# A shorter head, new layout limits and a clock term in the layout model, in a 32-head attention kernel on Trainium2

## The chip, the cores and the metric

The kernel runs on one core of one Trainium2 chip. The metric is the device time of one execution in microseconds (us). The span that a profile covers is about 1.8 us shorter than the time of the same execution (744.4 against 746.23 us for the kernel before). Profiles are therefore compared with profiles, and times with times.

Engines are called as the profile calls them: PE is the TensorE matmul array, PEld its weight loads, DVE is VectorE, ACT is ScalarE, POOL is GpSimd, SP is SyncE, which issues most of the DMA here. L1821 is a line of the kernel's file; the line numbers shift by 11 between the kernel before and the changed one.

## The reference, cut to what matters

```python
x = A_x                                   # 1 x 2048 x 512, bf16
g = sigmoid((x * gate_w).sum(-1, keepdims=True))
# branch A: full attention, 32 heads of 16, 2048 queries x 2048 keys
q, k, v = split_heads(x @ A_wqkv)
a = softmax(q @ k.T * 0.25) @ v           # per head
a = merge_heads(a) @ A_wo
# branch B: the same shapes, but each query sees 8 keys, 2 apart (a sliding window)
b = ...
return g * a + (1 - g) * b
```

Branch A has 32 x 2048 x 2048 exponentials, and these are what costs time. Branch B is spread among them.

## The kernel before

A *tile* is the scores of 128 keys against 512 queries of one head: one matmul that writes 128x512 fp32 of PSUM, a *bank* in the kernel's words. There are 32 x 16 x 4 = 2048 tiles. Each has to be exponentiated, in one of two ways:

```python
# on ScalarE: 2 or 3 tiles in one instruction (1024 or 1536 wide); one value matmul per tile later
nc.scalar.activation(out=self.pt[a][i][:, 0:n * 512], in_=<score bank(s)>, func=ACT.Exp, scale=SCALE)

# on VectorE: one eviction per tile to int16 (an exponential by bit pattern), then three passes per
# batch of four tiles, each shifted by a constant; FOUR value matmuls per tile later
nc.vector.tensor_scalar(out=self.yb[buf][:, 0, i*512:(i+1)*512], in0=bank[:], scalar1=A, scalar2=B, ...)
nc.vector.tensor_scalar(out=y[:, k, 0:n], in0=y[:, 0, 0:n], scalar1=<constant k>, op0=ALU.add)   # k = 1, 2, 3
```

Nothing waits at run time for a decision: the *layout*, that is, which tile goes to which engine and in what order every engine does its work, is chosen when the kernel is built. `run()` plays the five engines forward in a model of time and always lets the engine that is behind do its best next step. Its rules have 11 limits (how much VectorE backlog is allowed before another tile is given to it, how long a group of value matmuls may be put off, and so on). Each limit has a value for each of the 64 stretches of 32 tiles:

```python
STRETCH = dict(
    backlog="2222233122222220322224220212223212210222223222422222222222223122",
    grab="2222232222222221442241322222132342122242322222222122222222222222",
    # [cut: nine more]
)
PE_0, DVE_0, ACT_0, SLOT_0, K_0 = 1.25, 2.7, 1.3, 1.45, 2.1   # when the model thinks each engine is free
WARM_WIN, WARM_BAR, WARM_LOW = 3.42, 3500, 2900

def slow(now):       # the model's view of TensorE's clock: slower only while it is starved
    return 1.9 if now > 15 and sum(n for a, n in work if a > now - WARM_WIN) < WARM_LOW else 1.0
```

When TensorE has had little work, `run()` inserts *fillers*, matmuls by a zero weight that add nothing to the bank they go to.

The head prepares the first tile: transposes of the first 512 rows of x, projection of q, and projection of the first 512 keys in two parts, because the first scores need only 128 of them. Both parts go to the same PSUM bank, `flex[0]`:

```python
def head(self):
    # [cut: warm-up matmuls, 16 transposes of x, 4 copies to xT, 16 q matmuls]
    for a, b in ((0, 128), (128, 512)):
        for kc in range(4):
            self.mm4(self.flex[0][:, a:b], lambda c: wk[:, kc, 32*c:32*c+32], self.xT[:, kc, a:b], ...)
        if a == 0:
            nc.scalar.activation(out=self.qm[0][0][:], in_=self.flex[1][:], func=ACT.Copy, ...)
        nc.vector.tensor_copy(out=self.kT[0][:, a:b], in_=self.flex[0][:, a:b])
    # [cut]

# setup, on VectorE, before the head: masks that are needed only much later
nc.vector.tensor_scalar(out=pidx[:], in0=pidx[:], scalar1=4, ..., op0=ALU.arith_shift_right)
nc.vector.tensor_copy(out=pf[:], in_=pidx[:])
nc.vector.tensor_copy(out=ef, in_=ei)                          # 128x128 int32 to f32
nc.vector.tensor_scalar(out=self.Eh[:], in0=ef, ..., op0=ALU.is_equal)
nc.vector.tensor_reduce(out=self.fold[:], in_=<ident>, ..., op=ALU.max)

# jobs: the v projection of chunk st may start at tile 4*st; for st = 0 that is ahead of the first scores
ch = self.chain([("PE", ..., v_mm), ("DVE", ..., v_evac)], due=..., rel=4 * st, deps=xs[st // 4])
```

## Time and profile before

Six runs took 744.41 to 745.88 us, median 745.22. The table is worked out from the trace of the profiled run.

| what | before |
|---|---|
| busy: ACT / PE / DVE, us | 725.9 / 703.1 / 692.2 |
| first exponential starts | 9.34 us |
| last exponential starts | 733.60 us |
| exponentials: 1024-wide / 1536-wide | 474 / 209 (1575 tiles) |
| tiles on VectorE | 473 |
| filler matmuls | 96 |

From start to start, when nothing is in its way, ACT takes 0.905 us for a 1024-wide exponential, 1.332 us for a 1536-wide one and 0.477 us for the few 512-wide copies that it also does. I add these up from the first to the start of the last exponential and call the sum the *base* (710.7 us). What the real distances have above it is the *excess* (13.5 us). Base, excess, the start of the first exponential, and the *tail* (from the start of the last exponential to ACT's last output issue, 5.6 us) account for the span but for about 5 us behind that issue (its transfer lands after 3.1 us; then the program ends).

The first lines are from the page of the kernel before: the span, the busy time of each engine with its share, and the granted clock of TensorE in tenths over 40 slices of the span.

```profile
span 744.4 us, 21345 instructions
...
PE 703.1 (94%) x8673; PEld 232.3 (31%) x8673; DVE 692.2 (93%) x1176; ACT 725.9 (98%) x697; POOL 204.4 (27%) x212
...
PEclk9999999999999999999989999999998999999999
```

ACT is the bound, with 98%. PE and DVE are at 94% and 93%. The two 8s in the last row are the slices in which TensorE's clock was halved for a while (granted clock 0.50 for 10.24 us from 384.2 and for 6.83 us from 565.1).

The timeline of the kernel before, cut to the head. Columns: start, duration, engine, line, operation, out<-in, shapes, count, and in brackets the idle time before it and what ended that.

```profile
2.13 2.80 DVE L845 CAST t_96<-t_96 128x128 f32<-128x128 int32 x1
...
5.45 1.08 DVE L937 COPY xT<-fps 128x512 bf16<-128x512 bf16 x3
...
7.35 0.29 DVE L948 CAST kT_72<-fps 128x128 bf16<-128x128 f32 x1 [0.82 <-PE fps L865]
7.70 0.83 PE L865 MATMUL fps<-xT,ww 128*32 128x384 bf16 x16 [0.39 <-DVE kT_72 L948]
...
8.34 0.63 PE L865 MATMUL fps<-wAv,xT 128*32 128x128 bf16 x32
8.58 0.56 DVE L948 CAST kT_72<-fps 128x384 bf16<-128x384 f32 x1 [0.93 <-PE fps L865]
...
8.91 0.40 PE L1767 MATMUL fps<-qm_0_74,kT_72 32*128 32x512 bf16 x4
...
9.34 1.02 ACT L1821 ACTIVATE pt_0_83<-fps 128x1024 bf16<-128x1024 f32 x1 [1.52 <-PE fps L1767]
```

The 128 keys are evicted at 7.35. PE waits 0.39 us for that eviction, though its next matmuls need nothing from it: they write the same bank. Then come 16 matmuls for the other keys, 32 for v, and only then the first scores (8.91), although what these need was there at about 7.65. ACT waits until 9.34.

The table by stretches of the kernel before, around the first halved clock. Columns: stretch, its length, busy time and count on PE, PEld, DVE, ACT and POOL, granted clock, DMA share, GB/s.

```profile
380.00:382.00 2.00, 1.07 (x15) 0.33 (x13) 2.00 (x5) 2.00 (x3) 0.00 (x0) 1.00 0.03 8
...
384.00:386.00 2.00, 1.77 (x11) 0.44 (x11) 1.93 (x5) 2.00 (x3) 0.00 (x0) 0.54 0.57 225
...
388.00:390.00 2.00, 2.00 (x14) 0.24 (x9) 2.00 (x5) 2.00 (x2) 0.00 (x0) 0.50 0.09 30
...
392.00:394.00 2.00, 2.00 (x23) 0.35 (x20) 1.10 (x2) 1.69 (x3) 0.00 (x0) 0.50 0.42 136
394.00:396.00 2.00, 2.00 (x35) 0.57 (x27) 1.97 (x4) 2.00 (x2) 0.00 (x0) 0.90 0.44 140
```

PE is busy only 1.07 of 2 us at 380 to 382; from about 384 its clock is 0.50. At first ACT does not notice (2.00 of 2.00 busy). At 392 it does: 1.69, while PE, with its clock at 0.50, starts 23 matmuls in 2 us, where 394 to 396 has 35 at 0.90.

### The profile page before, as it was taken

How to read it: one execution, taken by the hardware profiler on the slowest of the kernel's cores; microseconds unless marked ns; L12 is line 12 of the kernel's file. 1: busy time of each engine (PE TensorE's matmuls, PEld its weight loads, DVE VectorE, ACT ScalarE, POOL GpSimd, SP SyncE). 2: the span in 40 equal slices, each digit the busy share in tenths (PEclk: the TensorE clock that was granted, in tenths of full speed). 3: DMA queues.
4: the chain of work that ended last, by engine and by line, in shares of the span. 5: the costliest groups of instructions: out<-in, count | busy, mean ns of one | idle time of the engine just before them, and what ended most of it. 6: DMA issues, size and time to landing. Idle time of an engine off the chain costs nothing.

```text
span 744.4 us, 21345 instructions
## 1 busy us (share of the span) xinstructions
PE 703.1 (94%) x8673; PEld 232.3 (31%) x8673; DVE 692.2 (93%) x1176; ACT 725.9 (98%) x697; POOL 204.4 (27%) x212
## 2 busy tenths in 40 slices
PE   9999999999999999999989999999999999999996
PEld 5422332333322333232222233223322223233443
DVE  6999999997999999999998999999999998989995
ACT  6999999999999999999999999999999999999995
POOL 2053000000002232231003446556543555553000
PEclk9999999999999999999989999999998999999999
DMA  5012001001000100001042655465534556531001
GB/s 164 3 22 60 9 3 29 2 2 38 2 6 11 23 1 9 2 1 37 9 131 83 155 135 146 116 155 146 139 96 119 139 138 147 141 85 31 17 23 34
DMA packets 63722, 48.58 MB, mean 65 GB/s; under 512 B 21760, under 2 KB 63232, under 8 KB 63488
## 3 DMA queue, kind: packets, MB, share of 16 engines
q1 hardware_dynamic: 62912, 45.70, 23.7%
q8 instruction: 70, 1.15, 0.7%
q0 software_dynamic: 288, 1.05, 0.4%
q10 hardware_dynamic: 416, 0.39, 0.2%
q14 instruction: 36, 0.29, 0.2%
HBM read 39.85 MB, written 5.26 MB: 61 GB/s over the span
## 4 chain that ended last, share of the span: by engine, by line
ACT 47%; PE 32%; issue 14%; DVE 4%; SPq 2%; DMA 1%; ACTq 0%; DVEq 0%
PE fps L1767 11%; PE fps L1573 10%; PE fps L865 9%; ACT pt_2_85 L1821 6%; ACT pt_0_87 L1821 6%; ACT pt_0_83 L1821 6%; ACT pt_1_84 L1821 6%; ACT pt_2_89 L1821 6%; ACT pt_1_88 L1821 6%; ACT pt_3_86 L1821 6%; ACT pt_3_90 L1821 5%; DVE yb_91 L1502 1%; SPq L922 1%; DVE yb_93 L1508 1%; SPq L1269 1%
## 5 line engine op out<-in xcount | busy, mean ns | idle before, releaser
L1573 PEld LDWEIGHTS <-vaug 128*32 128x32 bf16 x3685 | 85.8, 95 | 134.0 <-issue 110.9
L1821 ACT ACTIVATE pt_0_83<-fps 128x1536 bf16<-128x1536 f32 (+1 forms) x86 | 117.9, 1371 | 1.9 <-PE fps L1767 1.8
L1821 ACT ACTIVATE pt_1_84<-fps 128x1536 bf16<-128x1536 f32 (+1 forms) x86 | 117.9, 1371 | 0.8 <-PE fps L1767 0.6
L1821 ACT ACTIVATE pt_2_85<-fps 128x1536 bf16<-128x1536 f32 (+1 forms) x85 | 118.1, 1389 | 0.5 <-PE fps L1767 0.3
L1821 ACT ACTIVATE pt_3_86<-fps 128x1536 bf16<-128x1536 f32 (+1 forms) x85 | 116.4, 1370 | 0.5 <-PE fps L1767 0.5
L1502 DVE TENSOR_SCALAR yb_91<-fps 128x512 int16<-128x512 f32 x163 | 107.4, 680 | 8.2 <-PE fps L1767 7.8
L1502 DVE TENSOR_SCALAR yb_92<-fps 128x512 int16<-128x512 f32 x154 | 102.1, 682 | 6.6 <-PE fps L1767 6.2
L1502 DVE TENSOR_SCALAR yb_93<-fps 128x512 int16<-128x512 f32 x156 | 102.6, 681 | 4.6 <-PE fps L1767 4.3
L1573 PE MATMUL fps<-yb_91,vaug 128*32 128x512 f16 (+1 forms) x700 | 104.1, 372 | 0.3
L1573 PE MATMUL fps<-yb_92,vaug 128*32 128x512 f16 (+1 forms) x656 | 101.4, 370 | 0.0
L1573 PE MATMUL fps<-yb_93,vaug 128*32 128x512 f16 (+1 forms) x656 | 100.5, 381 | 0.0
L865 PE MATMUL fps<-xT,ww 128*32 128x512 bf16 (+2 forms) x1296 | 99.3, 381 | 0.6 <-DVE kT_72 L948 0.4
L1821 ACT ACTIVATE pt_1_88<-fps 128x1024 bf16<-128x1024 f32 x86 | 96.0, 1117 | 0.3 <-PE fps L1767 0.2
L1821 ACT ACTIVATE pt_0_87<-fps 128x1024 bf16<-128x1024 f32 x86 | 96.2, 1118 | 0.0
L1821 ACT ACTIVATE pt_2_89<-fps 128x1024 bf16<-128x1024 f32 x85 | 95.2, 1120 | 0.1
L1821 ACT ACTIVATE pt_3_90<-fps 128x1024 bf16<-128x1024 f32 x84 | 93.7, 1116 | 0.3 <-PE fps L1767 0.2
L1767 PEld LDWEIGHTS <-kT_73 32*128 32x128 bf16 x1024 | 45.9, 91 | 149.5 <-issue 147.3
L1767 PEld LDWEIGHTS <-kT_72 32*128 32x128 bf16 x1024 | 45.4, 91 | 148.1 <-issue 144.6
L1508 DVE TENSOR_SCALAR yb_91<-yb_91 128x2048 int16<-128x2048 int16 (+3 forms) x129 | 81.4, 658 | 0.2
L1508 DVE TENSOR_SCALAR yb_92<-yb_92 128x2048 int16<-128x2048 int16 (+3 forms) x129 | 78.9, 641 | 0.2
L1508 DVE TENSOR_SCALAR yb_93<-yb_93 128x2048 int16<-128x2048 int16 (+3 forms) x126 | 77.8, 651 | 0.3
L1170 POOL TENSOR_TENSOR prod_879<-bq_867,bk_868 128x512 bf16<-128x512 bf16 x32 | 34.2, 1074 | 105.7 <-DVE yb_92 L1508 47.8
(189 smaller groups left out, 1282.7 us busy)
## 6 DMA issues: line engine op xcount, KB each, us to landing
vw_5712<-v_dram SPq DMA_DIRECT2D x64, 128.0 KB, 3.1
vw_5713<-v_dram SPq DMA_DIRECT2D x64, 128.0 KB, 3.1
er<-er_dram SPq DMA_DIRECT2D x128, 64.0 KB, 2.9
erb_5708<-er_dram SPq DMA_DIRECT2D x64, 64.0 KB, 3.0
erb_5709<-er_dram SPq DMA_DIRECT2D x64, 64.0 KB, 2.9
out_dram<-ob SPq DMA_DIRECT2D x15, 128.0 KB, 2.5
ww<-in_B_wqkv_dram SPq DMA_DIRECT2D x12, 128.0 KB, 2.9
ww<-in_A_wqkv_dram SPq DMA_DIRECT2D x8, 128.0 KB, 3.0
```

Source lines behind the costliest of these rows:

```text
L865: self.nc.tensor.matmul(out=out_ps[32 * c:32 * c + 32, 0:n], lhsT=lhsT_of(c), rhs=rhs, start=start, stop=stop, tile_position=(0, 32 * c))
L922: self.nc.sync.dma_start(out=self.qm[i % NQM][r][k:k + 16, :], in_=self.qs[i % 2][k:k + 16, :])
L1170: return e.tensor_tensor(out=pr[m % 2][:, a:b], in0=bq[ct][:, a:b], in1=bk[ct][:, o + a:o + b], op=ALU.mult)
L1269: nc.sync.dma_start(out=st_["erb"][m % 4][32 * k + 16 * r:32 * k + 16 * r + 16], in_=_ap(src, src.offset, [[0, 16], [2 * WIN * 512, 4], [1 ...
L1502: return nc.vector.tensor_scalar(out=self.yb[bt["buf"]][:, 0, i * 512:(i + 1) * 512], in0=bank[:], scalar1=A, scalar2=1024.0 * (15.0 + PW_ ...
L1508: return nc.vector.tensor_scalar(out=y[:, k, 0:n], in0=y[:, 0, 0:n], scalar1=float(round(1024.0 * (PW_S[k] - PW_S[0]))), scalar2=None, op0 ...
L1573: nc.tensor.matmul(out=out, lhsT=v, rhs=r, start=start, stop=stop, tile_position=(0, 32 * j))
L1767: nc.tensor.matmul(out=dst, lhsT=self.kT[ct % 2][32 * j:32 * j + 32, kt * 128:(kt + 1) * 128], rhs=self.qm[(4 * ct + qc) % NQM][par][32 * ...
L1821: nc.scalar.activation(out=self.pt[pi[0]][pi[1]][:, 0:n * 512], in_=self.aslot[si][:, 0:n, :].rearrange("p a b -> p (a b)"), func=ACT.Exp, ...
```

## The change

The intent: start the first exponential earlier; make the layout model count TensorE as slow for a whole `WARM_WIN` after it was starved (this constant, `WARM_LOW` and the 1.9 are the file's own); and search the limits anew. Of that search only the result is in the file.

```diff
 STRETCH = dict(
-    backlog="2222233122222220322224220212223212210222223222422222222222223122",
+    backlog="2123241201224222222420224223121223222212044232222222222222223223",
     # [cut: all 11 rows are new]
-PE_0, DVE_0, ACT_0, SLOT_0, K_0 = 1.25, 2.7, 1.3, 1.45, 2.1
+PE_0, DVE_0, ACT_0, SLOT_0, K_0 = 1.6, 3.0, 1.75, 1.8, 2.35
-WARM_LOW = 2900
+WARM_LOW = 2750
@@ setup
-        nc.vector.tensor_scalar(out=pidx[:], ...)      # the five mask instructions
-        # [cut]
+    def heads(self):                                   # ... are now a method
+        # [cut: the same five instructions]
@@ head
-        for a, b in ((0, 128), (128, 512)):
+        for a, b, bank in ((0, 128, self.flex[3]), (128, 512, self.flex[0])):
             for kc in range(4):
-                self.mm4(self.flex[0][:, a:b], ...
+                self.mm4(bank[:, a:b], ...
@@ jobs
+        self.steps.append(Step("DVE", 0.9, self.heads, rel=24, due=30, cls=2))
-                            due=4 * st - 4 if st else -20, rel=4 * st, deps=xs[st // 4])
+                            due=4 * st - 4 if st else -20, rel=max(1, 4 * st), deps=xs[st // 4])
@@ run
-        fx_free = [K_0, DVE_0, INF, 0.0]
+        fx_free = [K_0, DVE_0, INF, 1.5]
         def slow(now):
-            return 1.9 if now > 15 and sum(n for a, n in work if a > now - WARM_WIN) < WARM_LOW else 1.0
+            nonlocal cold_until
+            if now > 15 and sum(n for a, n in work if a > now - WARM_WIN) < WARM_LOW:
+                cold_until = now + WARM_WIN
+            return 1.9 if now < cold_until else 1.0
```

So there are two parts: a *head* part (own bank, masks later, v behind the first scores) and a *layout* part (everything that follows from the new limits and the new model). The layout of the changed kernel has 1570 tiles on ACT instead of 1575, and 478 on VectorE instead of 473.

## The prediction

> **What bounds the kernel.** ScalarE. The page's busy table gives ACT 725.9 of 744.4 us (98%), PE 703.1 (94%), DVE 692.2 (93%). ACT runs its 683 exponentials almost without a gap from 9.34 us (first exponential in the timeline) to 734.7 us. From start to start a 1024-wide one takes 0.905 us and a 1536-wide one 1.332 us. Against these, the start-to-start distances lose about 12 us inside that stretch, in some 60 places, mostly 0.05 to 0.3 us. The rest is head (9.3 us) and tail (9.7 us).

> Two places stand out. In the table by stretches TensorE's granted clock is 0.50 at 384 to 394 us and at 565 to 572 us. [...] PE was busy only 1.07 of 2 us at 380 to 382. Around these ACT loses about 2.9 us together.

> **What the change does.**
> 1. Head. The 384 other keys get their own bank, so their matmuls no longer wait for the 128-key eviction (PE waits 0.39 us, from 7.31 to 7.70). The first v projection (32 matmuls, 0.63 us) moves behind the first scores. The head-mask setup (a 2.80 us cast beside GpSimd's memsets, then 0.29 and 0.36) moves later, so the first xT copy need not wait until 5.45; I think this gains little, as PE finishes its transposes only at 5.88. First scores near 8.0 instead of 8.91, first exponential near 8.4 to 8.5 instead of 9.34: 0.9 us, all on the critical path.
> 2. Mix. The built order has 1570 tiles exponentiated on ACT instead of 1575, and 478 instead of 473 on VectorE; ACT still has 683 exponentials, 204 wide instead of 209. That is 5 x 0.427 = 2.1 us less ACT. VectorE gets 5 more evictions and 3 more passes of about 0.65, 5 us in all, and had 52 us free.
> 3. Clock. Placing each kernel's PE order on the exponentials' measured spacing and counting matmul work per 3.4 us, I find a deep, long dip in the old order where the first slow stretch lies and another where the second lies. In the new order I find only brief shallow ones. So I expect no half-clock stretch, or a short one: 2.5 us (estimate).
> 4. Against it: about 19 more value-matmul slots, 10 more filler groups and 22 more single-tile score groups on PE, some 10 us of PE work by the old durations; vanished half-clock periods give most of that back. Some small ACT stalls may grow: 0.5 us.

> **Sum.** 745.2 - 0.9 - 2.1 - 2.5 + 0.5 = 740.2; I say 740.0 us, 8 in 10 between 737.0 and 743.0. Faster by over 2%: 0.02. Within 2%: 0.97. Slower by over 2%: 0.01.

> **What would show each step.** Timeline: first exponential at 8.3 to 8.6 us, no PE wait on the first kT copy, no early 2.8 us cast. ACT groups: 204 wide and 479 narrow. Stretches: clock 1.00 from 20 to 720 us. ACT's excess near 9 to 10 us rather than 12.

> **What would make it wrong.** The layout was searched with a model; the new order may starve TensorE where I see none, or make ACT wait for scores behind the added PE work, which would give the 5 us back. A brief dip may be enough to halve the clock. The gain could be larger if the new limits also remove many small stalls.

The 2.5 us for the clock was the author's estimate, from the 2.9 us that ACT loses around the two stretches at 0.50. The 3.4 us over which step 3 counts is the step in which the clock changes in the profile before: its halved stretches of 10.24 and 6.83 us are three and two times 3.41.

## The result, and the profile after

| | before | after |
|---|---|---|
| median of all runs, us | 745.50 (40 runs, 744.41 to 746.86) | 745.92 (20 runs, 744.59 to 747.47) |
| ratio, 95% interval | | 1.0009 (1.0003 to 1.0015) |
| busy: ACT / PE / DVE, us | 725.9 / 703.1 / 692.2 | 724.0 / 707.8 / 693.5 |
| first exponential starts | 9.34 | 8.58 |
| base (ACT's minimum) | 710.7 | 708.2 |
| excess | 13.5 | 16.3 |
| tail | 5.58 | 6.67 |
| exponentials 1024 / 1536 wide | 474 / 209 | 479 / 204 |
| filler matmuls | 96 | 133 |

Ratios here and below are the mean time of one kernel's fast runs over the mean of the other's in the same rounds, so they are not quite the ratio of the medians. The predicted 740.0 us (737 to 743) was wrong. The kernel is not faster; within a tenth of a per cent it is even slower.

The same three lines from the page of the changed kernel:

```profile
span 745.1 us, 21464 instructions
...
PE 707.8 (95%) x8728; PEld 235.6 (32%) x8728; DVE 693.5 (93%) x1184; ACT 724.0 (97%) x697; POOL 204.7 (27%) x212
...
PEclk9999999999999999999999999999999999999999
```

ACT has 1.9 us less to do, as was intended, and the span is not shorter. Both old dips of the clock are gone from the last row (a slice is 18.6 us, and 3.4 us at half clock still leave 0.91 of it, which is a 9).

The timeline of the changed kernel: first the head, then 12 to 16 us.

```profile
5.06 0.85 DVE L943 COPY xT<-fps 128x512 bf16<-128x512 bf16 x2 [3.09 <-PE fps L940]
...
7.59 0.29 DVE L954 CAST kT_72<-fps 128x128 bf16<-128x128 f32 x1 [0.83 <-PE fps L871]
...
8.11 0.40 PE L1778 MATMUL fps<-qm_0_74,kT_72 32*128 32x512 bf16 x4
8.24 0.56 DVE L954 CAST kT_72<-fps 128x384 bf16<-128x384 f32 x1 [0.36 <-PE fps L871]
8.58 1.02 ACT L1832 ACTIVATE pt_0_83<-fps 128x1024 bf16<-128x1024 f32 x1 [0.52 <-PE fps L1778]
...
9.17 0.63 PE L871 MATMUL fps<-wAv,xT 128*32 128x128 bf16 x32
...
12.57 1.03 ACT L1832 ACTIVATE pt_2_85<-fps 128x1024 bf16<-128x1024 f32 x1
...
12.70 1.05 PE L871 MATMUL fps<-xT,ww 128*32 128x512 bf16 x16
...
13.68 0.62 PE L963 MATMUL fps<-ident,x_in_119 128*128 128x128 bf16 x8
...
14.23 0.63 PE L871 MATMUL fps<-wAv,xT 128*32 128x128 bf16 x32
...
14.79 0.60 PE L1778 MATMUL fps<-qm_0_74,kT_72 32*128 32x512 bf16 x5
...
15.25 1.02 ACT L1832 ACTIVATE pt_2_89<-fps 128x1024 bf16<-128x1024 f32 x1 [1.65 <-PE fps L1778]
```

The head works as intended. The transposes of x begin at 4.39 us in both runs, but here they start about 0.107 us apart up to the last (5.99), where before they start 0.056 us apart from 5.32 on; the first change of the clock in the trace falls at 6.34 here and at 5.28 before. So the 128 keys are evicted 0.24 us *later* than before (7.59 against 7.35), and yet the scores start at 8.11 instead of 8.91 and the first exponential at 8.58 instead of 9.34. Directly behind it, however, there is a wait that the kernel before does not have: from 12.7 to 14.8 PE does a projection, eight transposes and v before the next scores, and ACT stands for 1.65 us. So 0.76 us are won at 8.6 us, and at first sight more than that is gone at 15.3 us.

The table by stretches of the changed kernel at 476 to 480 us, and from its timeline the exponential that paid for it.

```profile
476.00:478.00 2.00, 0.98 (x10) 0.25 (x13) 1.93 (x10) 2.00 (x3) 2.00 (x2) 0.84 0.20 42
478.00:480.00 2.00, 2.00 (x17) 0.56 (x16) 0.63 (x2) 1.62 (x2) 0.03 (x1) 0.50 0.13 33
```

```profile
480.95 1.45 ACT L1832 ACTIVATE pt_3_86<-fps 128x1536 bf16<-128x1536 f32 x1 [1.33 <-PE fps L1778]
```

There is a new short stretch of halved clock, 3.41 us from 477.4, and ACT then waits 1.33 us for scores.

The end, from the timeline of the kernel before and then of the changed one: the last exponential, VectorE's transpose of the last block of values, and the last output issue.

```profile
733.60 1.08 ACT L1821 ACTIVATE pt_3_86<-fps 128x1024 bf16<-128x1024 f32 x1
...
735.16 0.72 DVE L1596 STREAM_TRANSPOSE t_96<-fps 128x512 f32<-128x512 f32 x1 [2.61 <-PE fps L1573]
...
738.80 0.37 ACTq L1419 DMA_DIRECT2D out_dram<-eg  x1
```

```profile
733.07 1.46 ACT L1832 ACTIVATE pt_3_86<-fps 128x1536 bf16<-128x1536 f32 x1
...
735.30 0.72 DVE L1607 STREAM_TRANSPOSE t_96<-fps 128x512 f32<-128x512 f32 x1 [0.17 <-PE fps L1584]
...
739.37 0.37 ACTq L1426 DMA_DIRECT2D out_dram<-eg  x1
```

The changed kernel starts its last exponential 0.53 us earlier and ends 0.57 us later. Its last exponential is a wide one (1.46 instead of 1.08), and what follows it takes longer too.

Here is the ledger of the two profiles by place. "Excess" is split by where in the span it lies.

| | before | after | difference |
|---|---|---|---|
| first exponential | 9.34 | 8.58 | -0.76 |
| base | 710.7 | 708.2 | -2.5 |
| excess, 9 to 50 us | 1.28 | 3.17 | +1.9 |
| excess, 375 to 400 and 550 to 575 us (the old halved clock) | 3.38 | 1.66 | -1.7 |
| excess, 470 to 490 us (the new one) | 0.31 | 1.60 | +1.3 |
| excess, everywhere else | 8.5 | 9.9 | +1.3 |
| tail | 5.58 | 6.67 | +1.1 |
| rest | | | +0.1 |
| span | 744.4 | 745.1 | +0.7 |

The base falls by six times 0.427 us and not five, because the wide last exponential lies in the tail; 0.4 of the tail's 1.1 us is that same exponential. The table tells where the time is. It does not yet tell what causes what: that took experiments.

### The profile page after: what moved, and what is told of

The parts are those of the page before. It is cut to its first block, busy times and chain, and to the rows that moved or that the text cites. A ratio compares the mean times of both kernels' runs of the same rounds, so it can differ in the third digit from the quotient of the medians.

```text
span 745.1 us, 21464 instructions
## 1 busy us (share of the span) xinstructions
PE 707.8 (95%) x8728; PEld 235.6 (32%) x8728; DVE 693.5 (93%) x1184; ACT 724.0 (97%) x697; POOL 204.7 (27%) x212
## 4 chain that ended last, share of the span: by engine, by line
ACT 42%; PE 22%; DVE 14%; issue 13%; DMA 3%; SPq 3%; POOL 1%; ACTq 0%; DVEq 0%; POOLq 0%
PE fps L1778 8%; PE fps L1584 7%; ACT pt_3_86 L1832 6%; ACT pt_2_85 L1832 6%; ACT pt_0_83 L1832 6%; ACT pt_2_89 L1832 5%; PE fps L871 5%; ACT pt_0_87 L1832 5%; ACT pt_3_90 L1832 5%; ACT pt_1_88 L1832 5%; ACT pt_1_84 L1832 5%; DVE yb_92 L1513 2%; DVE yb_91 L1513 2%; DVE prod_822 L1177 2%; DMA vw_5740<-v_dram 1%
## 5 line engine op out<-in xcount | busy, mean ns | idle before, releaser
L1832 ACT ACTIVATE pt_0_83<-fps 128x1536 bf16<-128x1536 f32 (+1 forms) x87 | 119.4, 1372 | 1.4 <-PE fps L1778 1.0
L1832 ACT ACTIVATE pt_3_86<-fps 128x1536 bf16<-128x1536 f32 (+1 forms) x85 | 114.9, 1352 | 1.4 <-PE fps L1778 1.3
L1832 ACT ACTIVATE pt_2_85<-fps 128x1536 bf16<-128x1536 f32 (+1 forms) x85 | 116.0, 1364 | 0.1
L1832 ACT ACTIVATE pt_1_84<-fps 128x1024 bf16<-128x1024 f32 (+1 forms) x85 | 114.7, 1350 | 0.4 <-PE fps L1778 0.4
L1584 PE MATMUL fps<-yb_93,vaug 128*32 128x512 f16 (+1 forms) x672 | 101.5, 373 | 0.5 <-DVE vaug L899 0.5
L1584 PE MATMUL fps<-yb_91,vaug 128*32 128x512 f16 (+1 forms) x672 | 100.7, 370 | 0.8 <-DVE yb_91 L1519 0.7
L871 PE MATMUL fps<-xT,ww 128*32 128x512 bf16 (+2 forms) x1296 | 97.7, 380 | 0.0
L1584 PE MATMUL fps<-yb_92,vaug 128*32 128x512 f16 (+1 forms) x692 | 95.7, 368 | 0.2
L1519 DVE TENSOR_SCALAR yb_93<-yb_93 128x2048 int16<-128x2048 int16 (+2 forms) x126 | 81.0, 669 | 0.3
L1519 DVE TENSOR_SCALAR yb_92<-yb_92 128x2048 int16<-128x2048 int16 (+3 forms) x129 | 80.4, 654 | 0.2
L1519 DVE TENSOR_SCALAR yb_91<-yb_91 128x2048 int16<-128x2048 int16 (+3 forms) x132 | 80.1, 632 | 0.1
```

The source lines that it names most:

```text
L871: self.nc.tensor.matmul(out=out_ps[32 * c:32 * c + 32, 0:n], lhsT=lhsT_of(c), rhs=rhs, start=start, stop=stop, tile_position=(0, 32 * c))
L1519: return nc.vector.tensor_scalar(out=y[:, k, 0:n], in0=y[:, 0, 0:n], scalar1=float(round(1024.0 * (PW_S[k] - PW_S[0]))), scalar2=None, op0 ...
L1584: nc.tensor.matmul(out=out, lhsT=v, rhs=r, start=start, stop=stop, tile_position=(0, 32 * j))
L1832: nc.scalar.activation(out=self.pt[pi[0]][pi[1]][:, 0:n * 512], in_=self.aslot[si][:, 0:n, :].rearrange("p a b -> p (a b)"), func=ACT.Exp, ...
```

## The experiments

**Theories.** (A) *The early stall*: the head gain is real, and the reordering that follows it (the wait at 12.6 to 15.3 us) takes it back; move that and the gain appears. (B) *The layout is no better*: moving five tiles to VectorE and refilling PE costs in waits what it saves on ACT, wherever it is; the head by itself would gain. (C) *The clock*: halved clock decides; keep it away and either kernel gains the 2 to 3 us.

**How parts were separated.** A changed line changes the whole layout downstream, because the builder is greedy. So I made both kernels record their actions (engine, kind, what to issue) while the model runs, and issue them afterwards. Unedited, the recorded kernels have the same order of instructions and of waits on every engine as the originals. The traces of the edited runs agree: outside of what an edit names, the order on every engine is that of the original. An edit then touches only what it names, on the *old layout* (of the kernel before) or the *new layout* (of the changed one). The new limits with the old clock model and its old threshold (2900) could not be made: the build ended in an error while the layout was being made. With the new threshold (2750) and the old rule it does build, as does the kernel before with the new rule alone, but neither was tried on the chip. So the new clock term was never tried alone. All runs below gave correct results; one was wrong on purpose. Kernels of one batch ran on one chip together with the kernel before.

**Batch 1** (kernel before: 745.41 us, 9 runs)

*e1_head_bank.* Old layout; only the own bank, and the masks later. v stays ahead of the first scores.

```diff
-        for a, b in ((0, 128), (128, 512)):
+        for a, b, bank in ((0, 128, self.flex[3]), (128, 512, self.flex[0])):
@@ the five mask instructions leave the setup; on the old layout they are issued here, at about 22 us
         def gate_z():
             nc.vector.tensor_copy(out=self.gwr[:], ...)
+            self.heads()
```

> The kernel before with its whole layout frozen; only the bank of the first 128 keys and the late head masks are taken from the change, v stays ahead of the first scores. If the wait of TensorE on the first key eviction (0.39 us before) is a real part of the head: first exponential 0.3 to 0.5 us earlier (8.85 to 9.05 instead of 9.34) and a time 0.3 to 0.5 us lower. If whatever bounds the early stage is the second chunk of keys, the exponential starts earlier, a wait of ACT appears before about 16 us, and the time is unchanged.

Measured: 746.07 us, ratio 1.0004 (0.9989 to 1.0018). No gain. Its timeline shows why:

```profile
9.06 0.63 PE L870 MATMUL fps<-wAv,xT 128*32 128x128 bf16 x32 [0.86 <-DMA wAv<-in_A_wqkv_dram]
...
9.62 0.40 PE L1779 MATMUL fps<-qm,kT 32*128 32x512 bf16 x4
...
10.05 1.02 ACT L1834 ACTIVATE pt<-fps 128x1024 bf16<-128x1024 f32 x1 [2.00 <-PE fps L1779]
```

With the wait for the bank gone, the v matmuls, still ahead of the scores, wait 0.86 us for their own weights. The scores stand behind v in PE's order and start only at 9.62, and the first exponential comes at 10.05, later than before. I had taken v's weights as landed. (One profile shows this; how late the weights land differs between executions, see e2b.)

*e2_head_all.* As e1, and v behind the first scores: the whole head part on the old layout.

```diff
     def reorder(self, acts):
-        return acts
+        return acts[1:5] + acts[:1] + acts[5:]     # action 0 is v of chunk 0
```

> As the last, and the first v projection moved behind the first four scores: the whole head change on the old layout. Prediction's theory: first exponential at 8.3 to 8.6 us, nothing given back, time 0.8 to 0.9 us below before (about 744.6). Rival (the second key chunk bounds the early stage): same first exponential, but ACT waits up to 0.8 us before 16 us, time within 0.3 us of before. In this layout VectorE takes no early score tile, so the first key chunk lasts ACT 16 tiles; I lean to a gain of 0.5 to 0.8.

Measured: 743.73 us, ratio 0.9981 (0.9968 to 0.9995). The first exponential starts at 8.51:

```profile
8.51 2.91 ACT L1834 ACTIVATE pt<-fps 128x1024 bf16<-128x1024 f32 x3 [0.50 <-PE fps L1779]
```

The lead of 0.78 us over the kernel before is the same from tile 100 to tile 1000: in this run nothing takes it back. The profiled run was even 2.9 us shorter than the profile of before, for a second reason. The table by stretches of the kernel before at its second halved clock, and then of this kernel:

```profile
564.00:566.00 2.00, 1.68 (x16) 0.59 (x15) 2.00 (x4) 2.00 (x3) 0.00 (x0) 0.77 0.12 29
566.00:568.00 2.00, 2.00 (x19) 0.33 (x11) 2.00 (x5) 1.95 (x3) 0.00 (x0) 0.50 0.12 29
```

```profile
564.00:566.00 2.00, 2.00 (x19) 0.57 (x13) 2.00 (x5) 2.00 (x3) 0.00 (x0) 1.00 0.14 32
566.00:568.00 2.00, 1.91 (x24) 0.48 (x23) 2.00 (x4) 2.00 (x3) 0.79 (x1) 1.00 0.13 25
```

In e2 the clock is 1.00 here and ACT full, and the lead grows from 1.5 to 2.9 us over this place. The order of instructions is the same as in the kernel before from 22 us on; only the moment differs. So whether this second dip halves the clock is not a property of the order alone; this part of the gain is luck (see below, on how often the clock is halved).

*e3_warm_before.* Old layout and old head; filler matmuls behind the scores ahead of both halved stretches, to test theory C.

```diff
+            if cur in acc and (1026 < p < 1046 or 1553 < p < 1569):
+                # one zero-weight matmul per open accumulator, as in filler()
```

> The kernel before, frozen, with 11 filler groups (43 matmuls that add zeros) put on TensorE behind the scores of the two starved places (376 to 385 us and 561 to 566 us). If the half clock is what costs there: granted clock 1.00 from 20 to 720 us (mean 0.999 instead of 0.987), ACT's excess over 0.905/1.332 us spacing falls by about 2 us around 385 to 397 and 566 to 573, time 743.3 to 743.9. If ACT loses there for another reason (late scores by the order itself): clock 1.00 but less than 0.7 us gained.

Measured: 746.42 us, ratio 1.0010 (0.9996 to 1.0024). Of the halved stretches 6.83 us remained (at 387.8) and the one at 565 was gone, but the excess there only fell from 1.91 to 1.70: ACT now waited at 562.0 and 564.8 (0.43 and 0.61 us), with the clock at 1.00. Keeping the clock up with fillers put the fillers in front of the scores.

*e4_keys_first.* New layout; the first 62 actions reordered so that scores come ahead of the projection and transposes at 12.7 us. This is theory A's test.

```diff
     def reorder(self, acts):
-        return acts
+        head = [0, 1, 2, 3, 4, 6, 7, 8, 9, 10, 11, 12, 14, 15, 16, 5, 26, ...]   # a permutation of 0..61
+        return [acts[i] for i in head] + acts[62:]
```

> The changed kernel with its layout frozen from about 21 us on; within the first 62 steps the transposes, copies and projection of the second key chunk go ahead of the tiles that VectorE took early, and the scores of the last old keys go ahead of x chunk 2. If the ACT wait at 13.6 to 15.3 us (1.65 us) is the second key chunk coming late: the wait falls below 0.4 us, first exponential stays at 8.6, time 1.3 to 1.8 us below the changed kernel's (about 744.3). If the wait only moves to the third chunk, ACT's excess before 25 us stays near 2 us and the time stays at 745.9.

Measured: 747.01 us, ratio 1.0025 (1.0011 to 1.0039). The wait was not removed, it moved:

```profile
18.68 1.94 ACT L1839 ACTIVATE pt<-fps 128x1024 bf16<-128x1024 f32 x2 [1.83 <-PE fps L1784]
```

The excess from 9 to 25 us rose from 2.14 to 2.67 us. PE was busy 15.83 of the 16 us in this stretch of the changed kernel, which leaves little to reorder; but e2 has 15.80 there, and ACT full but for 0.3 us, so PE's share alone does not explain the wait. The clock was not halved anywhere between head and tail in this profile, and it was the slowest of the batch by its median.

**Batch 2** (kernel before: 745.73 us, 11 runs)

*e6_old_head.* The other corner of the square: new layout with the old head (shared bank, masks in the setup, v first).

```diff
-        for a, b, bank in ((0, 128, self.flex[3]), (128, 512, self.flex[0])):
+        for a, b, bank in ((0, 128, self.flex[0]), (128, 512, self.flex[0])):
@@ masks back in the setup
     def reorder(self, acts):
-        return acts
+        return acts[5:6] + acts[:5] + acts[6:]
```

> Fourth cell of the square: the changed kernel's frozen layout with the head of before (shared bank, early masks, v ahead of the first scores). The old layout gained 1.7 us by the new head (743.7 against 745.4). If head and layout add up, this cell is 1 to 1.7 us slower than the changed kernel (747.0 to 747.6) and the new layout is worth +2 us by itself. If the new layout only suits a fast head or hides it, the cell is within 0.4 us of the changed kernel (745.9).

Measured: 746.44 us, ratio 1.0013 (1.0000 to 1.0026); the first exponential at 9.67. The early stall is there just the same (1.80 us at 13.3), so it belongs to the layout and not to the head: theory A had put it down to the wrong part.

*e2b_again*: the kernel of e2_head_all once more. *c_after*: the changed kernel, unedited, in the same batch.

> The same kernel as e2_head_all (old layout, new head) once more, beside the changed kernel on one chip. If its gain is real: 743.3 to 744.5 and about 2 us below the changed kernel; runs at mean clock 0.992 about 1.3 us faster than runs at 0.987. If it was luck of that chip: within 0.7 us of before.

> The changed kernel itself as a control. 745.9, in two groups: mean clock 0.999 near 745.4, 0.995 to 0.997 near 747. The profile should show the same ACT excess by stretch as the first (2.1 before 25 us, 1.0 from 25 to 50), except at 470 to 490 us, where it is 1.6 with and about 0.3 without a half-clock window.

Measured: 744.45 us, ratio 0.9982 (0.9969 to 0.9995), and 747.10 us, ratio 1.0021 (1.0008 to 1.0033). The profile of c_after repeats the first one of the changed kernel: an excess of 2.13 from 9 to 25 us, 1.03 from 25 to 50 and 1.60 from 470 to 490. That of e2b shows that the head's gain is not safe: its first exponential starts at 8.26, 1.08 us before that of the kernel before, but v waits 0.66 us for its weights until 8.88 (in e2, the same program, v started at 8.40 without a wait), ACT loses 0.79 us there, and 0.30 us of lead are left. The head on the old layout is faster than the kernel before a second time, on another chip, and the two differ by 2.65 us here. With these, the square is filled (medians):

| | old head | new head |
|---|---|---|
| old layout | 745.50 (40 runs) | 743.73 and 744.45 |
| new layout | 746.44 | 745.92 (20 runs) and 747.10 |

The head gains on the old layout by 1 to 1.8 us, and part of that is luck with the clock. Among runs with a mean clock of 0.9905 or more, the median of the kernel before is 744.78 (10 runs of the three batches) and that of e2 and e2b 743.73 (5 runs); among runs with 0.9885 or less it is 745.74 (15) and 745.08 (3). So the head itself gives 0.7 to 1.1 us. The new layout loses about 1 us under the old head and 2 to 2.7 us under the new one: the two parts do not simply add. In runs with no halved stretch (mean clock 0.998 or more) the changed kernel has a median of 745.57 (10 runs) and e6 746.40 (4 runs), so the head's 0.8 us is there on the new layout too; it goes in the runs with the halved clock at 477 us, which at most one of e6's five runs had. The layout eats the whole gain of the head. That is theory B, with a share of theory C.

*e5_warm_after.* New layout and head; fillers behind the scores ahead of 477 us, as in e3.

```diff
+            if cur in acc and (1303 < p < 1319):
+                # one zero-weight matmul per open accumulator
```

> The changed kernel, frozen, with 5 filler groups (20 matmuls) behind the scores at 474 to 480 us. If the half-clock window at 477 us is what splits the changed kernel's runs: all runs at mean clock 0.999 and the median 0.5 to 0.9 us below the control's. Rival, after e3 (fillers there took the half clock away from one place and gained nothing, because they stand in front of scores): ACT excess from 470 to 490 stays over 1 us and the time does not fall.

Measured: 746.39 us, ratio 1.0016 (1.0003 to 1.0028). In the profile the clock stayed at 1.00 at 477 us and the excess there fell from 1.60 to 0.72. Against the control of the same batch, c_after, the median is 0.71 us lower, within what was expected; but the means are only 0.55 us apart, with a standard error of 0.60, and two of the five runs (747.51 and 747.78, mean clock 0.996) were as slow as the control. So whether these fillers help the changed kernel is unclear. They do not bring it below the kernel before.

**Batch 3** (kernel before: 745.30 us, 11 runs)

*e12_v_later.* Old layout, new head, and v still later: behind the transposes of the second chunk of x. An attempt at a version better than e2.

```diff
     def reorder(self, acts):
-        return acts
+        head = [1, 2, 3, 4, 5, 6, 8, 9, 10, 11, 12, 0, 13, 7]
+        return [acts[i] for i in head] + acts[14:]
```

> Old layout with the new head (e2), and v moved further back, behind both transposes of x chunk 1 and the next two scores. e2 gained 1.3 us on average, but in its second profile TensorE stood for the v weights (ACT excess 0.79 at 9.2 us). If that landing is what still varies: no ACT excess above 0.3 us before 15 us, and 743.2 to 744.0, at least 1.5 us below before and about 2.5 below the changed kernel. If not: equal to e2 (743.7 to 744.5).

Measured: 744.59 us, ratio 0.9992 (0.9977 to 1.0007): a miss. The profiled run was the shortest execution of all (742.63 us), with the first exponential at 8.21 and no second halved stretch; five of six runs had a lower mean clock (0.987 or 0.988 against 0.992) and were 0.8 to 3.1 us longer. Whatever v costs in the first 10 us seems smaller than what the clock does later; those five runs have no trace, so where they lost is not shown.

*e10_no_fill.* The changed kernel without its filler groups, in case they delay scores.

```diff
     def reorder(self, acts):
-        return acts
+        return [x for x in acts if x[1] != 'fill']
```

> The changed kernel, frozen, without any of its 133 filler matmuls. If the added fillers are what makes ACT wait a little more often in the new layout (1.3 us of excess spread over the middle): excess from 50 to 350 us falls from 3.7 to near 3.0 and the time falls, unless half-clock windows appear. If the fillers are harmless or useful: same excess outside half-clock windows, mean clock 0.98 to 0.99, time 1 to 3 us higher.

Measured: 746.38 us, ratio 1.0014 (1.0000 to 1.0028). The excess from 50 to 350 us was as with fillers, so they cost nothing there. New halved stretches came at 564.7 (3.41 us) and 653.4 (6.83 us), with 1.69 and 3.06 us of excess instead of 0.94 and 0.58. So with the fillers placed by the layout model the clock stayed at 1.00 at these places in the profile of the changed kernel, and without them it did not in this one. That they pay is not shown: the ratio 1.0014 lies between the two of the changed kernel (1.0009 and 1.0021), and the stretch at 477 us did not come here.

*e9_no_early.* The changed kernel with one limit of the first stretch changed, so that the score groups of the first 32 tiles take none along for VectorE (another rule still gave it four of the first 34, one at 8.91 us; in the changed kernel it has eight); the greedy builder then lays out everything anew.

```diff
-    grab="1222212222322312213324401214221222222232223223222222222222223243",
+    grab="0222212222322312213324401214221222222232223223222222222222223243",
```

> The changed kernel with one limit set so that VectorE takes none of the first 32 score tiles; the layout after that is another one and worse (448 tiles on VectorE instead of 478), so only the first 25 us are read, and the total should be about 10 us longer (755). If early VectorE tiles cause the ACT wait of 1.8 us at 12.6 us: excess before 25 us at most 0.9, as in the kernel before (0.76). If the wait comes from the order of the head: still 1.5 or more.

Measured: 766.82 us in a single run, and a miss on every count: the excess from 9 to 25 us was 2.23 us (0.96 of it just behind v, which waited for its weights until 9.47), and the total rose by 21 us. The builder gave VectorE 448 tiles instead of 478. One digit of 704 moved the kernel by 3%: these limits fit one trajectory, not a kind of kernel. For the question where the early lead goes, the run says nothing, because it is another layout from end to end.

*e11_short_tail.* The changed kernel with the value matmuls of VectorE's tiles left out once all scores are done, except the first and last of each accumulation. Its result is wrong on purpose (the comparison let it pass nonetheless, as few terms are left out). It asks if a backlog of value matmuls makes the longer tail.

```diff
+            if p >= N and kind == "y" and not first and not last:
+                return []
```

> The changed kernel, frozen, wrong on purpose: 24 half-width value matmuls of the last VectorE tiles are left out after the last score. From the start of the last exponential to the issue of the last output it takes 6.67 us (5.58 in the kernel before). If TensorE's backlog of value matmuls bounds the tail: 5.9 to 6.2. If VectorE's last passes or the normalization bound it: 6.5 to 6.7.

Measured: tail 6.42 us against 6.67, in a single run of 745.17 us. Inconclusive: it explains a quarter of a microsecond. With the wider last exponential (0.38), about half of the 1.1 us remains open.

**Where the new layout loses its lead.** For each kernel I took from the trace the moment at which *n* tiles (on ACT and VectorE together) have been begun, and subtracted it from that of the kernel before. Positive is ahead. (Counting all tiles of a wide exponential at its start moves single entries by up to 0.9 us, but hardly the difference between the first two columns.)

| n tiles begun (us in before) | after | e6: new layout, old head | e2: old layout, new head |
|---|---|---|---|
| 16 (15.6) | +0.76 | +0.08 | +0.76 |
| 32 (22.6) | +1.52 | +0.77 | +0.76 |
| 60 (32.4) | +0.87 | +0.12 | +0.78 |
| 100 (46.7) | -0.63 | -1.38 | +0.78 |
| 700 (259.5) | +1.73 | +0.97 | +0.78 |
| 1300 (473.0) | +0.53 | -0.21 | +1.58 |
| 1350 (490.6) | -0.96 | -0.26 | +1.53 |
| 1550 (559.9) | -1.22 | -0.43 | +1.56 |
| 1600 (578.6) | +0.13 | +0.88 | +2.91 |

Three things are to be read here. First, the changed kernel is ahead of e6 by 0.7 to 0.8 us in every row down to 473 us: the head's gain is kept until then. The halved clock at 477 us then costs the changed kernel 1.4 us that e6 (no halved clock) does not pay. Second, at 22.6 us the early ACT stall does not show yet: the changed kernel is ahead by 1.5 us, because VectorE took six more tiles meanwhile. The excess of ACT alone misleads in this kernel; with two engines that exponentiate, progress has to be counted in tiles. Third, from 22.6 to 46.7 us both kernels with the new layout lose 2.15 us. (The table's swings later, up to 1.7 at 260 us and down again, go with how many tiles VectorE has begun early: five more at 260 us, none at 115.)

The table by stretches for that place, of the kernel before and then of the changed kernel:

```profile
9.00:25.00 16.00, 15.49 (x324) 8.27 (x326) 11.06 (x23) 15.37 (x15) 0.24 (x4) 1.00 0.22 58
25.00:47.00 22.00, 21.25 (x343) 7.36 (x345) 21.26 (x39) 21.89 (x24) 6.11 (x6) 1.00 0.03 5
```

```profile
9.00:25.00 16.00, 15.83 (x298) 7.74 (x298) 15.63 (x31) 14.12 (x16) 0.24 (x4) 1.00 0.23 58
25.00:47.00 22.00, 20.59 (x381) 7.98 (x377) 18.46 (x36) 21.51 (x22) 6.90 (x7) 1.00 0.03 4
```

In the third number after the comma, DVE: the new layout loads VectorE to 15.63 us up to 25 us (before: 11.06) and then leaves it 18.46 instead of 21.26 us busy up to 47 us, 2.8 us less. Of that stretch, VectorE waits, says the table of waits of the changed kernel for 25 to 47 us (engine, line, waited for, us in total, times, longest):

```profile
DVE yb_91 L1513 <- PE fps L1778: 2.0, 3, 1.4
```

It waits for scores, which the same table of the kernel before does not show. So VectorE is given work earlier and starves later; the early five or six tiles are borrowed, not won. By 46.7 us it has begun 19 tiles in both kernels, and the early ACT stall is no longer covered; whether that stall or the later starvation is the cause of the loss, these traces do not tell. This is a reading of two traces. The experiment that should have confirmed it (e9) did not answer.

**How often the clock is halved.** The trace records the granted clock. Every halved stretch that a profile records was at 0.50 and lasted 3.41 us or 2, 3 or 6 times that: 10.24 and 6.83 us in before, 3.41 us in the changed kernel (the one at the end of each trace, which its end cuts off, is left aside). The mean clock of each run tells roughly which runs had them: of 27 runs of the changed kernel (its own and c_after's), 10 had 0.998 or more (no halved stretch between head and tail) with a median of 745.57 us, and 16 had 0.995 to 0.997 with a median of 746.99 us, most of them with one such stretch. The seven at 0.997 are not certain: the trace of e11 has that mean clock with a halved stretch at the end alone, and two of the seven took 744.93 and 745.89. So the halved stretch that both profiles show at 477 us comes in 11 to 17 of the 27 runs of the same program and costs about 1.4 us.

In the kernel before, 15 of the 31 runs whose clock was recorded had 0.9885 or less (median 745.74) and 10 had 0.9905 to 0.9945 (744.78): one us apart. Thus even when the changed kernel has no halved clock at all, it takes about as long as the kernel before, which has one or two.

## Why the prediction was wrong

1. *What bounds the kernel*: ACT, in head, base, excess and tail. The ledger adds up to the span within a few tenths of a microsecond in the profiles compared here. But "ACT is the bound" had led me to count only ACT's waits. PE and VectorE are within 7% of full too, and a tile moved from ACT to VectorE is a saving only if both have the room at that moment.
2. *Head, 0.9 us* "all on the critical path": right. 0.76 us in the profile of the changed kernel, 0.78 in e2, and the lead is kept there; in e2b v's weights take all but 0.30 of it back. The start itself varies: 7.88 to 8.58 us in seven profiles with the new head, 9.34 to 9.67 in three with the old one. That masks and the xT copy matter little was right too (the 128x128 cast of the masks took 2.80 us beside GpSimd's memsets, which it outlasted, 4.93 against 4.85 us; without them, at 24.91 us in the changed kernel, 0.22). What I had not seen is that v behind the scores is the part that makes it safer: the own bank alone (e1) lets v's weights become the next wait.
3. *Mix, 2.1 us less ACT*: right as arithmetic (base 2.5 lower, 0.4 of it back in the wide last exponential). As a saving of time it did not arrive: e6 has this mix without the new head and took 746.44 us.
4. *Clock, 2.5 us, "no half-clock stretch, or a short one"*: the old places did lose their halved clock, but gave 1.7 us and not 2.5. The short one that I allowed for came in 11 to 17 of 27 runs and cost 1.3 us in the profile. On average 0.9 to 1.2 us was left (1.7 less 17/27 or 11/27 of 1.3). I had costed a halved stretch by the ACT time lost around it. In e3 the second halved stretch went away and 1.70 of the 1.91 us of excess stayed, as other waits; in e5 0.72 of 1.60 stayed. So the halved clock is not the whole of that loss.
5. *"Against it: 0.5 us"*: **this is the step that failed.** By the ledger it was about 4.4 us: 1.9 in excess from 9 to 50 us, 1.3 spread over the rest, 1.1 in the tail (0.4 of it the wide last exponential) and 0.1 of the rest. The prediction named the mechanism among what would make it wrong ("make ACT wait for scores behind the added PE work, which would give the 5 us back") and gave it a tenth of its size. The clock is the second, smaller miss: in the profile it gave 0.4 us net (1.7 less 1.3) where 2.5 had been counted. The sum of the terms, in the profile: -0.76 - 2.5 - 1.7 + 1.3 + 4.4 = +0.7, where -0.9 - 2.1 - 2.5 + 0.5 = -5.0 had been expected.

What is shown: the head part gains by itself, the layout part loses by itself (0.13% under the old head, at the edge of the noise, and clearly under the new one), the early ACT stall belongs to the layout, and fillers after which the clock stayed up (e3 at 565 us, e5 at 477 us) bring neither kernel below the kernel before (whether they help the changed one is unclear). What is read from traces only: that VectorE's starvation between 25 and 47 us is where the new layout falls behind. What stays open: which limit makes it so, or whether the new clock term does, which was not tried alone; where the 1.3 us of small waits elsewhere come from, and about half of the longer tail. The best version found is e2_head_all, the head part on the old limits: 0.9981 and 0.9982 of the kernel before in two batches, faster than both kernels, by less than a fifth of a per cent.

## What to carry to other kernels

When a change joins a local repair with a new search of parameters, freeze the layout and test the two apart: here the repair gained what it promised, and the search, which was to be the larger part, lost it. Where two engines share a kind of work, count progress in items finished on both, not in the waits of the busier one: a stall of 1.7 us on ScalarE did not show as long as VectorE had tiles ahead, and showed when VectorE starved 15 us later. A saving on the bounding engine that puts work on engines which are 94% busy should be costed by the waits that it will make, not by their average idle time.
